# Routing and list matmuls in the routing's own PSUM bank, list steps on VectorE, weight preparation off GpSimd

## The chip, the cores and the metric

The kernel runs on one core of one Trainium2 chip. The metric is the device time of one execution in microseconds. PE is TensorE, DVE is VectorE, ACT is ScalarE, POOL is GpSimd, SP is SyncE (it issues most DMAs).

## The reference

Three parts follow one another. Attention over 4 batches and 8 heads gives x, 2304 tokens by 512. A gated hidden layer gives x2 = ((x·w1) * (x·w2))·w3·w_out, with 1024 hidden units. Then each token goes to one of 8 experts, at most 288 tokens each, in the order of all logits:

```python
logits = x @ w_gate
order = np.argsort(-logits.flatten())
for idx in order:
    tok, e = divmod(int(idx), E)
    if assigned[tok] >= 0 or counts[e] >= cap:
        continue
    assigned[tok] = e
    counts[e] += 1
for e in range(E):
    out[assigned == e] = np.maximum(x[assigned == e] @ w1[e], 0) @ w2[e]
```

The matrices are multiplied as two parts, a rounded high one and the rest (`xhi`, `xlo`, `wh`, `wl`), in three matmuls: high·high, low·high, high·low.

## The kernel before

Attention takes the first 511 us. From 512 to 775 us lies the hidden layer ("h"): for each of 8 slices of 128 hidden units, `weights` (line 1241) prepares w1 and w2, `split_x` (line 1255) splits x, and `hidden` (line 1289) forms a·b. A weight arrives as 64-bit words. `convert` rebuilds it in 128x512 pieces (`cv_raw`, `cv_v`): one DVE tensor_scalar, two DVE bit operations, one POOL multiply (a square, 40 of them in the program), and a DVE compare against `LEAST` squared that puts tiny values to zero. `split` then rounds the high part on ACT or DVE and subtracts the low part on DVE or POOL, whichever a planner finds free. Beside the h slices run the steps of `project` (`wo`, `og`), the product of the gate with the later weights, from which the logits come.

From 723 to 821 us PE forms W = w3·w_out (`pb<-wo,w`), and from 821 to 940 us x2 = h·W in 18 tiles of 128 tokens, each 24 matmuls of 512 columns. The last LATE = 3 tiles are made in two halves of 256 columns; the left halves first, so that expert 0's tokens can be gathered early. From 945 us the experts run: gather, first layer (e1), second layer (e2), scatter.

Between these matmuls run the routing and the lists. `routing` (line 872) has 8 phases. In each of the first 7 it looks for a threshold in 4 rounds; a round is a chain that alternates between DVE and PE: DVE makes `rt_mask`, PE counts (`rt_oh,rt_mask`, three matmuls), DVE makes `rt_cnt` and `rt_own`, PE adds over partitions (`rt_own,rc_ones`), DVE reduces. After the fourth round come `rt_rows` (PE: `rc_neg`, `rc_neg`, `rc_tri`), a scan, `rt_y`, and the choice of tokens that ends in the next `rt_oh`. `slot_lists` (line 1098) then makes one expert's list of tokens beside the next phase's first round: `sl_all`, `sl_rows`, a matmul with `rc_tris`, `sl_pre`, the slot of each token, `sl_oh` (one-hot rows, 3 DVE operations of 128x576), `sl_mv`, and 18 matmuls whose stationaries are 96 columns of `sl_oh`.

What sets the order: class `Sched` (line 163) plans all engines before the program is built, from modelled durations and priorities; each engine then runs its list in order. Small DVE temporaries of routing and lists lie in one PSUM bank (`in_bank`, line 853), named pt_68 in the order's rows. The results of routing and list matmuls go to one of three other PSUM tiles, pt_65 to pt_67 ("slots", through `Hold`), which the transposes of gathered tokens use as well. The trace writes all four as `pt`. Line 113 is the helper through which most instructions are recorded.

Of the kernel before, what the change touches and what calls it, by code (L numbers as in the profile page):

```python
# [775 lines left out]
def routing_consts(nc, pool, spare):  # L776
# [69 lines left out]
    c["g4"] = g4 = pool.tile([128, 4], F32, name="rc_first")  # L846
    nc.gpsimd.iota(g4, pattern=[[96, 4]], base=1, channel_multiplier=0, allow_small_or_imprecise_dtypes=True)
# [24 lines left out]
def routing(nc, sch, rp, slots, bank, c, L, keyL, A, rows_of, idx, prio, prio_l):  # L872
# [6 lines left out]
    def ring(name, n, shape, dt):  # L879
        return make_ring(sch, rp, "rt_" + name, n, shape, dt)  # L880
# [16 lines left out]
    r_al, r_acc, r_s = at("al", 1, [128, 8], F32), ring("acc", 1, [128, 8, NC], F32), at("s", 1, [128, NC], F32)  # L897
# [29 lines left out]
    for ph in range(8):  # L927
# [19 lines left out]
        if ph < 7:  # L947
# [4 lines left out]
            for rd, b in enumerate(BITS):  # L952
# [19 lines left out]
                ps = Hold(slots)  # L972

                def f(ps=ps, mask=mask, oh=oh):
# [17 lines left out]
                ps = Hold(slots)  # L992
                sch.op("PE", 110, lambda ps=ps: nc.tensor.matmul(
                    ps.tile[:, 0:NTHR * 8], c["ones16"], own8.rearrange("p t e -> p (t e)"), start=True, stop=True), r=["own8", "own8r"],
                    takes=ps, prio=prio, slack=RT_SLACK)
                dve(NTHR * 8, lambda ps=ps, any_=any_: nc.vector.tensor_reduce(
                    any_, ps.tile[:, 0:NTHR * 8].rearrange("p (t e) -> p t e", e=8), axis=AX.X, op=OP.max), [], [kany], uses=[ps])
# [32 lines left out]
            ps = Hold(slots)  # L1030

            def f(ps=ps, rows=rows):
                nc.tensor.matmul(ps.tile[:, 0:8], c["neg"], rows[:, 0:8], start=True, stop=True)
                nc.tensor.matmul(ps.tile[:, 8:16], c["neg"], rows[:, 0:8], start=True, stop=False)
                nc.tensor.matmul(ps.tile[:, 8:16], c["tri"], rows[:, 8:16], start=False, stop=True)
            sch.op("PE", 40, f, r=[kro], takes=ps, prio=prio)
# [9 lines left out]
            sch.op("DVE", c_dve(8), lambda ps=ps, r2=r2: nc.vector.tensor_tensor(r2, ps.tile[:, 0:8], rem, op=OP.add),  # L1046
                   r=[keyR], uses=[ps], w=[kr2], prio=prio)
# [4 lines left out]
            sch.op("DVE", c_dve(8), lambda ps=ps, al=al: nc.vector.scalar_tensor_tensor(  # L1052
                al, ps.tile[:, 8:16], 1e6, rem, op0=OP.add, op1=OP.add), r=[keyR], uses=[ps], w=[kal], prio=prio)
# [8 lines left out]
            ac2, kac2 = r_acc()  # L1062
# [6 lines left out]
            dve(144, lambda ac2=ac2: nc.gpsimd.tensor_tensor(A, A, ac2, op=OP.add), ["A", kac2], ["A"], "POOL")  # L1069
# [28 lines left out]
def slot_lists(nc, sch, rp, slots, bank, c, A, idx, prio, prio_l):  # L1098
# [8 lines left out]
    r_inc, r_pre, r_slot = ring("inc", 2, [128, NC], F32), ring("pre", 2, [128, 1], F32), at("slot", 2, [128, NC], F32)  # L1107
    r_ge, r_g, r_r = ring("ge", 2, [128, NC, 4], F32), ring("g", 2, [128, NC], F32), at("r", 1, [128, NC], F32)
    r_oh, r_og = ring("oh", 1, [128, NC, 96], BF16), ring("og", 1, [128, NC, 3], F32)
    r_mv, r_fl = ring("mv", 2, [128, 2, 3, NC], BF16), ring("fl", 2, [96, 2, 3], F32)  # L1110

    def lists(n, own):
# [15 lines left out]
        ps = Hold(slots)  # L1128
        sch.op("PE", 60, lambda: nc.tensor.matmul(ps.tile[:, 0:1], c["tris"], rows, start=True, stop=True),
               r=[kr], takes=ps, prio=prio_l)  # L1130
        dve(36, lambda: nc.vector.tensor_tensor_scan(inc, c["rst"][:, 0, :], s, 0.0, op0=OP.mult, op1=OP.add), [ks], [ki])
        dve(1, lambda: nc.vector.tensor_copy(pre, ps.tile[:, 0:1]), [], [kp], uses=[ps])
        dve(18, lambda: nc.vector.scalar_tensor_tensor(slot, inc, pre, s, op0=OP.add, op1=OP.mult), [ki, kp, ks], [ksl])
        dve(72, lambda: nc.vector.tensor_tensor(
            ge, slot[:, :, None].to_broadcast([128, NC, 4]), c["g4"][:, None, :].to_broadcast([128, NC, 4]), op=OP.is_ge),
            [ksl], [kg])
        dve(54, lambda: nc.vector.tensor_reduce(g, ge[:, :, 0:3], axis=AX.X, op=OP.add), [kg], [kc])
        dve(18, lambda: nc.vector.scalar_tensor_tensor(r, g, -96.0, slot, op0=OP.mult, op1=OP.add), [kc, ksl], [krr])
        for x in range(3):
# [13 lines left out]
        sch.op("PE", 18 * 60, f2, r=[(ko, x) for x in range(3)] + [(km, x) for x in range(2)], takes=ps2, prio=prio_l, slack=LIST_SLACK)  # L1153
        dve(6, lambda: nc.vector.tensor_copy(fl.rearrange("p x g -> p (x g)"), ps2.tile[:96, 0:6]), [], [kf], uses=[ps2])
# [14 lines left out]
def moe_and_experts(tc, sch, env, w1, w2, w3, w_out, w_gate, e1, e2, out):  # L1169
# [44 lines left out]
    def convert(w, row, col, blocks, width, pr):  # L1214
# [3 lines left out]
        if w.dtype != mybir.dt.int64:  # L1218
# [95 lines left out]
    def logits(f, c, pr):  # L1314
# [4 lines left out]
        split(lambda: hh[:, :], lambda: hl[:, :], lambda: hraw[:, f, cs], LC, pr, h_keys(f, c * LC, LC), khh, khl)  # L1319
# [20 lines left out]
    def project(nm, weight, copy, rows_n, cols, stat, stat_key, put_hi, put_lo, dst_key, step):  # L1340
# [4 lines left out]
        for t in range(n):  # L1345
            ac = slice(128, 256)
            for h in range(cols // DM):
                pr = P_WG + WG_STEP * (step + t * (cols // DM) + h)
                v, kv = convert(weight, t * 128, h * DM, 1, DM, pr)
                if nm == "og":  # L1350
# [3 lines left out]
                                   key, (key, 1), free=free))  # L1354
# [148 lines left out]
    r_xo = ring(xr, "x2o", 3, [128, DM], F32)  # L1503
# [268 lines left out]
LATE = 3  # L1772
# [57 lines left out]
```

## Time and profile before

| | |
|---|---|
| time, median of 3 runs | 1218.14 us (1217.03 to 1221.08) |
| profiled execution | 1218.05 us, its span 1216.1 us |
| mean granted clock of PE | 0.986 of full speed |
| busy: PE, DVE, ACT, POOL | 95%, 80%, 54%, 50% of the span |
| chain that ended last | PE 77%, DVE 15%, DMA 3%, issue 2% |

PE is busy for 1159.5 us of the span and idle for 56.6 us. A row of the timeline gives start, duration, engine, line, the operation and, in brackets, how long the engine was idle just before and what ended that. Matmuls overlap, so the distance of two starts says more than a duration.

### The profile page before, as it was taken

How to read it: one execution, taken by the hardware profiler on the slowest of the kernel's cores; microseconds unless marked ns; L12 is line 12 of the kernel's file. 1: busy time of each engine (PE TensorE's matmuls, PEld its weight loads, DVE VectorE, ACT ScalarE, POOL GpSimd, SP SyncE). 2: the span in 40 equal slices, each digit the busy share in tenths (PEclk: the TensorE clock that was granted, in tenths of full speed). 3: DMA queues.
4: the chain of work that ended last, by engine and by line, in shares of the span. 5: the costliest groups of instructions: out<-in, count | busy, mean ns of one | idle time of the engine just before them, and what ended most of it. 6: DMA issues, size and time to landing. Idle time of an engine off the chain costs nothing.

```text
span 1216.1 us, 24258 instructions
## 1 busy us (share of the span) xinstructions
PE 1159.5 (95%) x8377; PEld 1093.1 (90%) x8377; DVE 976.6 (80%) x2930; ACT 655.7 (54%) x1365; POOL 613.9 (50%) x645
## 2 busy tenths in 40 slices
PE   7999999999999999889999999999999799899996
PEld 6899999999999999879999999877768799899996
DVE  8899999999999999998777777677777877867541
ACT  6788888888888888642222220214222454444520
POOL 4566666666666665644423334323443368766110
PEclk9999999999999999999999999999999799999998
DMA  8576666666666653125455542544112564445520
GB/s 210 141 175 156 155 158 143 154 158 145 154 143 154 159 115 87 39 87 183 174 180 176 175 146 70 158 159 137 37 44 50 168 213 160 164 145 168 190 71 20
DMA packets 114217, 167.91 MB, mean 138 GB/s; under 512 B 47479, under 2 KB 77310, under 8 KB 114094
## 3 DMA queue, kind: packets, MB, share of 16 engines
q1 hardware_dynamic: 110926, 156.92, 47.5%
q0 software_dynamic: 3168, 9.44, 2.5%
q8 instruction: 66, 1.08, 0.4%
q14 instruction: 57, 0.47, 0.1%
HBM read 104.87 MB, written 22.48 MB: 105 GB/s over the span
## 4 chain that ended last, share of the span: by engine, by line
PE 77%; DVE 15%; DMA 3%; issue 2%; SPq 1%; POOL 1%; ACT 1%; DVEq 0%; POOLq 0%; ACTq 0%
PE pb L113 37%; PE s L590 12%; PE pt L614 7%; PE pt L664 6%; PE pt L113 6%; PE s L664 5%; DVE pt L113 3%; PE s L614 3%; DVE cv_v L113 2%; DMA u<-in_moe_w_dram 1%; DVE p L600 1%; DVE p_lo L648 1%; PE pt L543 1%; DVE sl_oh L113 1%; DMA cv_raw<-in_moe_w_dram 1%
## 5 line engine op out<-in xcount | busy, mean ns | idle before, releaser
L600 DVE TENSOR_SCALAR_CACHE_REDUCE p<-s 128x384 f32<-128x384 f32 x432 | 229.8, 550 | 35.9 <-PE s L590 12.3
L590 PE MATMUL s<-kst,qst 128*128 128x384 f32 x768 | 200.8, 361 | 5.5 <-DVE p L600 3.1
L605 ACT ACTIVATE p<-p,mn 128x1152 f32<-128x1152 f32 x144 | 181.1, 1258 | 26.1 <-DVE mn L603 23.9
L113 PE MATMUL pb<-xhi,wh 128*128 128x288 f32 x512 | 155.4, 304 | 1.7 <-ACT wh L113 1.7
L113 PE MATMUL pb<-xlo,wh 128*128 128x288 f32 x512 | 151.3, 296 | 4.0 <-DVE xlo L113 3.8
L113 PE MATMUL pb<-xhi,wl 128*128 128x288 f32 x512 | 150.9, 295 | 1.4 <-DVE wl L113 1.4
L590 PEld LDWEIGHTS s<-kst,qst 128*128 128x128 f32 x768 | 124.3, 192 | 11.4 <-DVE p L600 7.6
L614 PE MATMUL pt<-ident,p 128*128 128x128 f32 x879 | 132.1, 272 | 0.3 <-ACT p L605 0.3
L648 DVE TENSOR_TENSOR p_lo<-pt,p_hi 128x384 fp32r<-128x384 f32 x230 | 124.5, 551 | 0.8 <-ACT p_hi L331 0.7
L331 ACT ACTIVATE p_hi<-pt 128x384 fp32r<-128x384 f32 x230 | 106.6, 493 | 11.9 <-PE pt L614 10.2
L614 PEld LDWEIGHTS pt<-ident,p 128*128 128x128 f32 x879 | 106.8, 140 | 4.4 <-ACT p L605 0.5
L113 DVE SCALAR_TENSOR_TENSOR cv_v<-cv_raw,cv_v 128x512 int32<-128x512 int32 (+1 forms) x120 | 102.1, 856 | 7.1 <-POOL cv_raw L113 4.9
L113 PEld LDWEIGHTS pb<-xlo,wh 128*128 128x128 f32 x512 | 96.2, 188 | 5.0 <-DVE xlo L113 4.9
L113 PEld LDWEIGHTS pb<-xhi,wh 128*128 128x128 f32 x512 | 96.1, 188 | 2.5 <-ACT wh L113 1.9
L113 PEld LDWEIGHTS pb<-xhi,wl 128*128 128x128 f32 x512 | 96.1, 188 | 1.8 <-DVE wl L113 1.8
L341 POOL TENSOR_TENSOR p_lo<-praw,p_hi 128x384 fp32r<-128x384 f32 x96 | 96.8, 1016 | 0.4
L113 ACT ACTIVATE a<-pb 128x288 f32<-128x288 f32 x64 | 26.3, 410 | 131.3 <-PE pb L113 125.1
L335 POOL CAST p_hi<-praw 128x384 fp32r<-128x384 f32 x96 | 47.5, 505 | 84.8 <-ACT praw L331 84.8
L113 POOL TENSOR_TENSOR ul<-u,uh 128x1024 fp32r<-128x1024 f32 (+1 forms) x41 | 77.1, 1904 | 21.8 <-ACT uh L113 21.8
L113 POOL TENSOR_TENSOR cv_raw<-cv_raw 128x512 f32<-128x512 f32 x40 | 43.2, 1079 | 87.0 <-DVE cv_v L113 67.8
L113 PE MATMUL pb<-exh,uh 128*128 128x288 f32 x248 | 79.9, 322 | 0.0
L113 PE MATMUL pb<-ehh,uh 128*128 128x288 f32 x256 | 79.4, 310 | 0.0
(316 smaller groups left out, 3293.7 us busy)
## 6 DMA issues: line engine op xcount, KB each, us to landing
u<-in_moe_w_dram SPq DMA_DIRECT2D x64, 512.0 KB, 3.7
cv_raw<-in_moe_w_dram SPq DMA_DIRECT2D x32, 512.0 KB, 4.1
vr<-in_v_dram SPq DMA_DIRECT2D x32, 288.0 KB, 5.5
kr<-in_k_dram SPq DMA_DIRECT2D x32, 288.0 KB, 5.7
kst<-kH SPq DMA_DIRECT2D x31, 288.0 KB, 3.9
kst<-kL SPq DMA_DIRECT2D x31, 288.0 KB, 5.4
qr<-in_q_dram SPq DMA_DIRECT2D x15, 576.0 KB, 5.3
w3t<-wg SPq DMA_DIRECT2D x16, 512.0 KB, 3.5
```

The source lines that it names most:

```text
L113: return f(*[x.get() if isinstance(x, Lazy) else x for x in a], **{n: x.get() if isinstance(x, Lazy) else x for n, x in k.items()})
L331: nc.scalar.activation(out, in_, AF.Copy)
L335: nc.gpsimd.tensor_copy(out, in_)
L341: (nc.vector if eng == "DVE" else nc.gpsimd).tensor_tensor(out, a, b, op=OP.subtract)
L543: nc.tensor.transpose(ps.tile[:, a * 128:(a + 1) * 128], r[:, 3 * c + a, :, :].rearrange("p h d -> p (h d)"), ident)
L590: nc.tensor.matmul(ps.tile[:, :384], a[:, :], b[:, cs], start=(n == 0), stop=(n == len(passes) - 1))
L600: sch.op("DVE", c_dve(384), lambda ps=ps, c=c, cs=cs: nc.vector.tensor_scalar(t[:, cs], ps.tile[:, :384], 1.0, BIG, op0=OP.mult, op1=OP.mi ...
L605: sch.op("ACT", c_act(S, psum=False, acc=True), lambda: nc.scalar.activation(t, t, AF.Exp, bias=mn[:, 3:4], scale=-1.0, accum_out=sm[0][:, ...
L614: nc.tensor.transpose(ps.tile[:, a * 128:(a + 1) * 128], t[:, b * 128:(b + 1) * 128], ident)
L648: sch.op("DVE", c_dve(384), lambda view=view, src=src: nc.vector.tensor_tensor(view(lo), src(), view(hi).bitcast(F32), op=OP.subtract), us ...
L664: nc.tensor.matmul(ps.tile[:, :n], vt[:, t, :, :], src[half][:, t, off:off + n], start=(half == 0 and t == 0), stop=(half == 1 and t == NT ...
```

## The change

- `convert`: the POOL square becomes an absolute value on ACT; the compare is against `LEAST`.
- Splits of the hidden layer, of `wo` and of h: high parts on ACT only, low parts on DVE only (the first slice's `wl` and the first batch's `xlo` may still go to POOL, the first batch's `xhi` to DVE). `project` starts with the second slice, at a rate of 0.6 steps per chunk rather than 0.5.
- LATE is 4 rather than 3.
- List steps: the addition to `A`, `og` and the two `sl_mv` go from POOL to DVE; `sl_ge` has 54 elements rather than 72 and reads two SBUF tiles; `sl_oh` gets 32 zero columns, and each of the 18 list matmuls reads 128 columns.
- All routing and list matmuls write into the routing's bank rather than into a slot.

```diff
 # routing
-                ps = Hold(slots)
-                        nc.tensor.matmul(ps.tile[0:NCG * NTHR, 0:NCG * 8], mask[:, gs, :].rearrange("p a t -> p (a t)"),
+                pc, kpc = r_pcnt()
+                        nc.tensor.matmul(pc, mask[:, gs, :].rearrange("p a t -> p (a t)"),
...
+            pr_, kpr = r_prows()
+                nc.tensor.matmul(pr_[:, 0:8], c["neg"], rows[:, 0:8], start=True, stop=True)
...
-            dve(144, lambda ac2=ac2: nc.gpsimd.tensor_tensor(A, A, ac2, op=OP.add), ["A", kac2], ["A"], "POOL")
+            dve(144, lambda ac2=ac2: nc.vector.tensor_tensor(A, A, ac2, op=OP.add), ["A", kac2], ["A"])
 # slot_lists
+        pb, kpb = r_before()
+        sch.op("PE", 60, lambda: nc.tensor.matmul(pb, c["tris"], rows, start=True, stop=True),
...
-        dve(54, lambda: nc.gpsimd.tensor_tensor(og, ge[:, :, 0:3], ge[:, :, 1:4], op=OP.subtract), [kg], [kog], engine="POOL")
+        dve(54, lambda: nc.vector.tensor_tensor(
+            og, g[:, :, None].to_broadcast([128, NC, 3]), c["g4"][:, None, 3:6].to_broadcast([128, NC, 3]), op=OP.is_equal), [kc], [kog])
...
-                nc.tensor.matmul(ps2.tile[:96, 0:6], oh[:, k, :], mv[:, :, :, k], start=(k == 0), stop=(k == NC - 1))
+                nc.tensor.matmul(pl[:, :], oh[:, k * 96:k * 96 + 128], mv[:, :, :, k], start=(k == 0), stop=(k == NC - 1))
 # convert, split, project
-        sch.op("POOL", c_pool(n), lambda: nc.gpsimd.tensor_tensor(
-            raw[:, :, 0].bitcast(F32), raw[:, :, 1].bitcast(F32), raw[:, :, 1].bitcast(F32), op=OP.mult), r=[kv], w=[kr], prio=pr)
+        sch.op("ACT", c_act(n, False), lambda: nc.scalar.activation(raw[:, :, 0].bitcast(F32), raw[:, :, 1].bitcast(F32), AF.Abs),
...
-        split(..., khh, khl)
+        split(..., khh, khl, hi_e=("ACT",), lo_e=("DVE",))
...
-            if int((f * NCH + c + 1) * WG_RATE) > int((f * NCH + c) * WG_RATE):
+            if f and int((f * NCH + c + 1) * WG_RATE) > int((f * NCH + c) * WG_RATE):
...
-PRE_UNITS, MAIN_UNITS, LG_LAG, WG_RATE = 4, 9, 6, 0.5
+PRE_UNITS, MAIN_UNITS, LG_LAG, WG_RATE = 4, 9, 6, 0.6
-LATE = 3
+LATE = 4
```

The order on the engines changes with it, from the hidden layer on; attention's stays, but for its last operations. First the second list on DVE, at the first round's count; what an instruction waits for stands in brackets, pt_65 to pt_67 are the slots and pt_68 is the routing's bank. Before:

```order
L113 SCALAR_TENSOR_TENSOR rows_10030<-pt_68,rc_row 128x4 [waits DVE_49]
L113 TENSOR_TENSOR rt_pend_9186<-rt_pend_9186,pt_68 128x8
L113 TENSOR_TENSOR sl_all_9586<-A,pt_68 128x144 [waits Pool_49]
L113 TENSOR_TENSOR rt_cnt_9245<-pt_67,rc_diag 90x48 [waits PE_49]
L113 TENSOR_REDUCE pt_68<-sl_all_9586 128x18 [waits DVE_49]
L113 TENSOR_REDUCE pt_68<-rt_cnt_9245 90x8 [waits DVE_49]
L113 TENSOR_REDUCE sl_rows_10046<-pt_68 128x1 [waits DVE_49]
L113 SCALAR_TENSOR_TENSOR sl_inc_10048<-rc_rst,pt_68 128x18
L113 TENSOR_TENSOR rt_own_9188<-pt_68,rc_thr 90x120
L113 COPY sl_pre_10055<-pt_66 128x1 [waits PE_49]
L113 SCALAR_TENSOR_TENSOR pt_68<-sl_inc_10048,sl_pre_10055,pt_68 128x18 [waits DVE_49]
L113 TENSOR_TENSOR sl_ge_10062<-pt_68,rc_first 128x72 [waits DVE_49]
```

and in the changed kernel:

```order
L113 SCALAR_TENSOR_TENSOR rows_10033<-pt_68,rc_row 128x4 [waits DVE_49]
L113 TENSOR_TENSOR rt_pend_9188<-rt_pend_9188,pt_68 128x8 [waits PE_49]
L113 TENSOR_TENSOR sl_all_9591<-A,pt_68 128x144
L113 TENSOR_TENSOR rt_cnt_9249<-pt_68,rc_diag 90x48
L113 TENSOR_REDUCE pt_68<-sl_all_9591 128x18 [waits DVE_49]
L113 TENSOR_REDUCE pt_68<-rt_cnt_9249 90x8 [waits DVE_49]
L113 TENSOR_REDUCE sl_rows_10051<-pt_68 128x1 [waits DVE_49]
L113 SCALAR_TENSOR_TENSOR sl_inc_10054<-rc_rst,pt_68 128x18
L113 TENSOR_TENSOR rt_own_9190<-pt_68,rc_thr 90x120
L113 COPY sl_pre_10060<-pt_68 128x1 [waits PE_49]
L113 SCALAR_TENSOR_TENSOR sl_slot_10064<-sl_inc_10054,sl_pre_10060,pt_68 128x18 [waits PE_49]
L113 TENSOR_REDUCE pt_68<-pt_68 128x15 [waits DVE_49]
```

The order is the same, but `rt_pend` and the slot's operation, which touch the bank and use no result of PE, now wait for PE as well: the first for the count, the second for the sum of `rt_own`.

Next PE at the change from x2 to expert 0, the fourth list. Before:

```order
L113 LDWEIGHTS rt_mask_9215
L113 MATMUL pt_65<-rt_oh_9232,rt_mask_9215 90x48
L113 LDWEIGHTS rc_ones_145
L113 MATMUL pt_67<-rt_own_9188,rc_ones_145 128x120 [waits DVE_49]
L113 LDWEIGHTS rc_tris
L113 MATMUL pt_66<-sl_rows_10046,rc_tris 128x1 [waits DVE_49]
L113 MATMUL pt_65<-ident,early 128x96 [waits DMASW0_49]
L113 MATMUL pt_65<-ident,early 128x96 [waits DMASW1_49]
```

and in the changed kernel:

```order
L113 LDWEIGHTS rt_mask_9221
L113 MATMUL pt_68<-rt_oh_9236,rt_mask_9221 90x48
L113 LDWEIGHTS rc_tris
L113 MATMUL pt_68<-sl_rows_10051,rc_tris 128x1 [waits DVE_49]
L113 LDWEIGHTS rc_ones_145
L113 MATMUL pt_68<-rt_own_9190,rc_ones_145 128x120 [waits DVE_49]
L113 MATMUL pt_65<-ident,early 128x96 [waits DMASW0_49]
L113 MATMUL pt_65<-ident,early 128x96 [waits DMASW1_49]
```

The matmuls on `sl_rows` and `rt_own` have changed places and now write to pt_68; the transposes of `early` follow as before.

Last POOL from the end of attention into the hidden layer. Before:

```order
L113 TENSOR_TENSOR cv_raw_6159<-cv_raw_6159 128x512
L113 TENSOR_TENSOR cv_raw_6191<-cv_raw_6191 128x512
L738 TENSOR_TENSOR x_101<-x_101,rs_207 128x576
L113 MEMSET wg_hl 128x1408
L113 TENSOR_TENSOR xlo_6573<-x_94,xhi_6564 128x576
L113 TENSOR_TENSOR cv_raw_6159<-cv_raw_6159 128x512
L113 TENSOR_TENSOR cv_raw_6191<-cv_raw_6191 128x512
L113 TENSOR_TENSOR hl_6625<-hraw,hh_6601 128x384
L113 TENSOR_TENSOR wl_6639<-cv_v_6300,wh_6628 128x512
L113 TENSOR_TENSOR hl_6660<-hraw,hh_6633 128x384
```

and in the changed kernel:

```order
L113 TENSOR_TENSOR wl_6457<-cv_v_6301,wh_6450 128x512
L738 TENSOR_TENSOR x_101<-x_101,rs_208 128x576
L113 MEMSET wg_hl 128x1408
L113 TENSOR_TENSOR x2l_9186<-hraw,x2h_9172 128x512 x2
L113 TENSOR_TENSOR x2l_9233<-hraw,x2h_9195 128x512
L113 TENSOR_TENSOR Wl<-wt_9215,Wh 128x512
```

The squares (`cv_raw`) and the `hl`, `xlo` and `wl` of this stretch are gone from POOL, but for one `wl`; its next work after `wg_hl` is that of x2 and W.

## Rows read from the trace of the kernel before

**Rows 1.** Windows: busy of PE, PEld, DVE, ACT, POOL; clock; DMA share; GB/s.

```profile
512.00:548.00 36.00, 29.27 (x209) 27.35 (x210) 34.84 (x48) 14.01 (x27) 19.38 (x14) 1.00 0.27 90
775.00:821.00 46.00, 43.75 (x215) 32.84 (x215) 33.38 (x139) 9.65 (x16) 15.00 (x15) 1.00 0.53 170
821.00:906.00 85.00, 79.29 (x416) 59.80 (x416) 63.95 (x251) 27.12 (x47) 35.21 (x34) 1.00 0.28 75
906.00:975.00 69.00, 59.04 (x422) 53.09 (x421) 53.54 (x180) 25.21 (x45) 25.63 (x25) 0.90 0.37 108
```

**Rows 2.** Waits of PE, 511 to 548 us: total us, times, longest us.

```profile
PE pb L113 <- DVE xlo L113: 3.8, 3, 1.7
PE pb L113 <- ACT wh L113: 1.7, 1, 1.7
PE pb L113 <- DVE wl L113: 1.4, 2, 1.1
```

**Rows 3.** Waits of PE, 775 to 1216 us, the same columns.

```profile
PE pt L113 <- DVE rt_oh L113: 6.8, 6, 2.0
PE pt L113 <- DVE rt_mask L113: 6.0, 6, 3.3
PE pt L113 <- DVE exl L113: 5.0, 3, 2.6
PE pt L113 <- DVE sl_rows L113: 3.5, 4, 1.7
PE pt L113 <- DVE rt_own L113: 2.8, 3, 2.0
```

**Rows 4.** Groups of DVE, 505 to 546 us: busy, mean ns, idle before.

```profile
L113 DVE SCALAR_TENSOR_TENSOR cv_v<-cv_raw,cv_v 128x512 int32<-128x512 int32 x12 | 13.1, 1100 | 0.1
L113 DVE CAST xhi<-x 128x576 fp32r<-128x576 f32 x3 | 3.8, 1267 | 0.0
```

**Rows 5.** Timeline of DVE, one instruction of that stretch: start us, us, instruction.

```profile
508.34 0.69 DVE L113 SCALAR_TENSOR_TENSOR cv_v<-cv_raw,cv_v 128x512 int32<-128x512 int32 x1
```

**Rows 6.** Timeline of DVE around the second list: start us, us, instruction, [idle before <-releaser].

```profile
851.62 0.20 DVE L113 TENSOR_TENSOR rt_cnt<-pt,rc_diag 90x48 f16<-90x48 f32 x1 [0.63 <-PE pt L113]
...
855.79 0.30 DVE L113 SCALAR_TENSOR_TENSOR rt_y<-rt_ge,pt 128x144 f32<-128x144 f32 x1
...
856.01 0.16 DVE L113 TENSOR_TENSOR rt_r<-pt,rt_rem 128x8 f32<-128x8 f32 x1
...
860.51 0.29 DVE L113 TENSOR_TENSOR rt_oh<-rt_t,pt 128x144 bf16<-128x144 f32 x1
...
861.52 0.16 DVE L113 SCALAR_TENSOR_TENSOR rows<-pt,rc_row 128x4 int32<-128x4 f32 x1
...
862.92 0.25 DVE L113 TENSOR_TENSOR rt_own<-pt,rc_thr 90x120 f16<-90x120 f32 x1
...
868.07 0.44 DVE L113 TENSOR_TENSOR rt_mask<-pt,rt_thr 128x270 bf16<-128x270 f32 x1
```

**Rows 7.** Timeline of PE in the same stretch.

```profile
855.52 0.20 PE L113 MATMUL pt<-rt_rows,rc_neg 128*128 128x8 bf16 x2
...
860.85 0.27 PE L113 MATMUL pt<-rt_oh,rt_mask 128*90 128x48 bf16 x3 [0.85 <-DVE rt_oh L113]
...
862.96 0.16 PE L113 MATMUL pt<-sl_rows,rc_tris 128*128 128x1 bf16 x1 [0.61 <-DVE sl_rows L113]
...
867.11 0.95 PE L113 MATMUL pt<-sl_mv,sl_oh 128*96 128x6 bf16 x18
...
868.56 0.31 PE L113 MATMUL pt<-rt_oh,rt_mask 128*90 128x48 bf16 x3 [0.50 <-DVE rt_mask L113]
```

**Rows 8.** Weight loads of two tiles: ns min/median/max, starts, forms.

```profile
L113 PEld LDWEIGHTS <-sl_oh x144: 121/126/197, 822.5 to 1114.0; 128*96 128x96 bf16 x144
L113 PEld LDWEIGHTS <-rc_neg x14: 95/98/101, 811.1 to 1092.7; 128*128 128x128 bf16 x14
```

**Rows 9.** Timeline of DVE, one instruction of the fifth list.

```profile
1060.20 3.75 DVE L113 SCALAR_TENSOR_TENSOR idx<-sl_fl 96x3 int32<-96x3 f32 x1
```

More of the change, by code (lines that the diff above doesn't have):

```diff
@@ L991, in routing @@
                     c["thr"][:, :, None].to_broadcast([NCG * NTHR, NTHR, 8]), op=OP.mult), [ksm], ["own8"])
[L992 to L997, printed above, removed]
+                pa, kpa = r_pany()
+                sch.op("PE", 110, lambda pa=pa: nc.tensor.matmul(
+                    pa, c["ones16"], own8.rearrange("p t e -> p (t e)"), start=True, stop=True), r=["own8", "own8r"],
+                    w=[kpa], prio=prio, slack=RT_SLACK)
+                dve(NTHR * 8, lambda pa=pa, any_=any_: nc.vector.tensor_reduce(
+                    any_, pa.rearrange("p (t e) -> p t e", e=8), axis=AX.X, op=OP.max), [kpa], [kany])
                 dve(NTHR, lambda any_=any_, flag=flag: nc.vector.tensor_scalar(flag, any_, 0.0, None, op0=OP.is_ge), [kany], [kf])
@@ L1029, in routing, with f @@
             dve(288, f, [(kge, 0), (kge, 1)], [kro])
[L1030 to L1036, printed above, removed]
+            pr_, kpr = r_prows()
+            def f(pr_=pr_, rows=rows):
+                nc.tensor.matmul(pr_[:, 0:8], c["neg"], rows[:, 0:8], start=True, stop=True)
+                nc.tensor.matmul(pr_[:, 8:16], c["neg"], rows[:, 0:8], start=True, stop=False)
+                nc.tensor.matmul(pr_[:, 8:16], c["tri"], rows[:, 8:16], start=False, stop=True)
+            sch.op("PE", 40, f, r=[kro], w=[kpr], prio=prio, slack=RT_SLACK)
             inc, kin = r_incp()
@@ L1127, in lists @@
         dve(18, f, [ks], [kr])
-        ps = Hold(slots)
-        sch.op("PE", 60, lambda: nc.tensor.matmul(ps.tile[:, 0:1], c["tris"], rows, start=True, stop=True),
-               r=[kr], takes=ps, prio=prio_l)
+        pb, kpb = r_before()
+        sch.op("PE", 60, lambda: nc.tensor.matmul(pb, c["tris"], rows, start=True, stop=True),
+               r=[kr], w=[kpb], prio=prio_l, slack=LIST_FIRST)
         dve(36, lambda: nc.vector.tensor_tensor_scan(inc, c["rst"][:, 0, :], s, 0.0, op0=OP.mult, op1=OP.add), [ks], [ki])
-        dve(1, lambda: nc.vector.tensor_copy(pre, ps.tile[:, 0:1]), [], [kp], uses=[ps])
+        dve(1, lambda: nc.vector.tensor_copy(pre, pb), [kpb], [kp])
         dve(18, lambda: nc.vector.scalar_tensor_tensor(slot, inc, pre, s, op0=OP.add, op1=OP.mult), [ki, kp, ks], [ksl])
-        dve(72, lambda: nc.vector.tensor_tensor(
-            ge, slot[:, :, None].to_broadcast([128, NC, 4]), c["g4"][:, None, :].to_broadcast([128, NC, 4]), op=OP.is_ge),
+        dve(54, lambda: nc.vector.tensor_tensor(
+            ge, slot[:, :, None].to_broadcast([128, NC, 3]), c["g4"][:, None, 0:3].to_broadcast([128, NC, 3]), op=OP.is_ge),
             [ksl], [kg])
-        dve(54, lambda: nc.vector.tensor_reduce(g, ge[:, :, 0:3], axis=AX.X, op=OP.add), [kg], [kc])
+        dve(54, lambda: nc.vector.tensor_reduce(g, ge, axis=AX.X, op=OP.add), [kg], [kc])
         dve(18, lambda: nc.vector.scalar_tensor_tensor(r, g, -96.0, slot, op0=OP.mult, op1=OP.add), [kc, ksl], [krr])
@@ L1246, in weights @@
             split(lambda wh=wh, x=x: wh[:, x].rearrange("p k c -> p (k c)"), lambda wl=wl, x=x: wl[:, x].rearrange("p k c -> p (k c)"),
-                  lambda v=v: v.bitcast(F32), 512, pr, [kv], (kwh, x), (kwl, x))
+                  lambda v=v: v.bitcast(F32), 512, pr, [kv], (kwh, x), (kwl, x), hi_e=("ACT",), lo_e=("DVE", "POOL") if sch.label == "cv" else ("DVE",))
         return (wh, kwh), (wl, kwl)
@@ L1259, in split_x @@
             hi, free = xhi[i]
-            pages.first(sch.op(None, {"ACT": c_act(SP, False), "DVE": c_dve(SP, fast=True)},
+            pages.first(sch.op(None, {"ACT": c_act(SP, False)} | ({"DVE": c_dve(SP, fast=True)} if b == 0 else {}),
                                lambda eng, i=i, hi=hi: evac(eng, hi[:, :], xT[i][:, :]), r=[("x", b, k)], w=[("xhi", b, k)] + free,
                                prio=pr))
-            sch.op(None, {"DVE": c_dve(SP), "POOL": c_pool(SP)}, lambda eng, i=i, k=k, lo=lo, hi=hi: sub(
+            sch.op(None, {"DVE": c_dve(SP)} | ({"POOL": c_pool(SP)} if b == 0 else {}), lambda eng, i=i, k=k, lo=lo, hi=hi: sub(
                 eng, lo[:, k, :], xT[i][:, :], hi[:, :].bitcast(F32)), r=[("x", b, k), ("xhi", b, k)], w=[("xlo", b, k)], prio=pr)
@@ L1318, in logits @@
         hl, khl = r_hl()
-        split(lambda: hh[:, :], lambda: hl[:, :], lambda: hraw[:, f, cs], LC, pr, h_keys(f, c * LC, LC), khh, khl)
+        split(lambda: hh[:, :], lambda: hl[:, :], lambda: hraw[:, f, cs], LC, pr, h_keys(f, c * LC, LC), khh, khl, hi_e=("ACT",), lo_e=("DVE",))
         o0 = LW - 16 - 16 * c
@@ L1353, in project @@
                     tt.first(split(lambda hl=hl: hl[:, 0, :], lambda hl=hl: hl[:, 1, :], lambda v=v: v.bitcast(F32), DM, pr, [kv],
-                                   key, (key, 1), free=free))
+                                   key, (key, 1), hi_e=("ACT",), lo_e=("DVE",), free=free))
                     store(copy[t], hl, [key, (key, 1)], [(nm, "f", t)], pr)
```

64 lines of the change are left out of this document (36 added, 28 removed).

## The prediction

> **What bounds the kernel now.** I read the stages first, by windows, then what PE waited for, then the timeline of one list. PE is busy nearly everywhere, so what counts is where it is not. In 512 to 548 us, the start of the hidden layer, PE works 29.3 of 36 us while DVE works 34.8 of them [rows 1]: DVE bounds that stretch. PE waits there 3.8 us for `xlo`, 1.7 for `wh`, 1.4 for `wl`, together 6.9 [rows 2]. From 775 us on the routing's chain shows: PE is idle for 2.3, 5.7 and 10.0 us in the three next windows, and in the last of these its granted clock is 0.90 [rows 1]. The waits for `rt_oh`, `rt_mask`, `sl_rows` and `rt_own` make 6.8 + 6.0 + 3.5 + 2.8 = 19.1 us; expert 0's tokens (`exl`) make 5.0 [rows 3]. Those 19.1 us lie almost all beside lists: a plain round is covered by the matmuls placed around it.
>
> **The change, part by part.**
>
> *Start of the hidden layer.* Twelve DVE bit operations took 1.10 us on average there, three casts of `xhi` 1.27 us each [rows 4], while the same bit operation with POOL idle took 0.69 us [rows 5]. POOL's squares and low parts leave the stretch, so 12 x 0.41 = 4.9 us come off DVE, and the casts, 3.8 us, go to ACT. Against that DVE gets POOL's few low parts, each about the size of one bit operation: five of them are 3.5 us. DVE comes out some 5 us ahead in a stretch where PE waited 6.9 us for it. The later start of `project` takes DVE work out as well, which I count against the weight chain that no longer overlaps. I take -5.5 us; the ends are 0 (the chain to the first `wh` is one of latency) and -6.9 (all waits gone). Later in this layer DVE has room, and what moves to it and to ACT costs nothing; if that cover were gone it would show as waits for `hl` or `wl`.
>
> *List matmuls of 128 columns.* A list's 18 matmuls take 0.95 us [rows 7], and their weight loads of 96 columns 126 ns each, where a load of 128 columns takes 98 ns [rows 8]. By that ratio a list takes 0.74 us: 8 x 0.21 = 1.7 us saved. The ends are 0 and half of the 0.95, 3.8 us in all. I take -1.7, the row's own ratio. The Trainium skill, "TensorE: Matmul & The Clock Gate", section "Weight-path perf modes — Fast Weight Load (FWL) and DoubleRow", says that loads become about twice as fast where there are 128 weight columns and the type is not fp32. The trace agrees in sign (98 ns against 126 ns); by the factor of two the term would be -3.8 us, and the sum 1225.
>
> *One bank.* In the changed order a PE matmul that writes to the routing's bank waits for the last DVE instruction before it that touches this bank, and the next DVE instruction that touches it waits for the matmul, whether or not the data are related. In a plain round the chain alternates anyway and nothing is added. Beside a list two chains share the bank. I work the second list through:
> - The matmuls on `rt_rows` started at 855.52 us and their reader `rt_r` at 856.01, hidden by the scan before `rt_y` [rows 6, 7]. Now they wait for the scan's end (about 855.76) and `rt_y` waits for them: PE stalls 0.3 us, and `rt_y` starts at 856.3 rather than 855.79, 0.5 later.
> - The addition to `A` on DVE: 0.3 us, as `rt_y`, which has the same size [rows 6].
> - The count behind `rt_oh` waits for `rows`, which ends at 861.68 rather than 860.80 [rows 6]: 0.9 later. So the count moves from 860.85 to 862.55. PE has one x2 matmul more before it (18 took 4.4 us between 855.6 and 860.0, 0.24 each [rows 7]). Its wait grows from 0.85 to 2.0 us.
> - Then `rt_pend` waits for the count, 0.63 us as `rt_cnt` did [rows 6]; from the end of `rows` to that of `rt_own` it was 1.5 us, so `sl_rows` finds PE idle for 0.65 us, as before (0.61 [rows 7]).
> - `sl_pre` waits for that matmul, the matmul on `rt_own` waits for `sl_pre` (PE idle 0.45), and the slot waits for that one: two trips of 0.63 us that were hidden. From the end of `rt_own` to that of `rt_mask` it was 5.3 us [rows 6]; with 1.3 for the trips and 0.65 for `og` and two `sl_mv` (each like a small DVE row, 0.16 to 0.25) it is 7.25. PE has 20 matmuls, 4.7 us, instead of 15 and the list: it waits 1.65 rather than 0.50 us.
> - The next `rt_cnt` waits for the whole list, with three matmuls behind it on PE: about 0.5 us.
>
> Together 0.3 + 2.0 + 0.65 + 0.45 + 1.65 + 0.5 = 5.55 us of stalls instead of 1.96, so +3.5 a list. Three lists lie beside W and x2: +10.5. At the fourth, PE has 15 matmuls of 256 columns before the count instead of 23, and none between count, `sl_rows` and `rt_own`; some of the `exl` waits should go, as slots come free and the early gather has four tiles of right halves for cover instead of three. Net +2.5. At the fifth and sixth the matmuls of the experts are the cover; I take +2 each. The last two have no rounds beside them: 0. Sum +17; the ends are 0 and 7 x 3.5 = +24.5. DVE is the waiting engine each time; behind its waits stand the splits of x2 or of the experts, and PE waits for these no sooner than for the routing.
>
> The Trainium skill, "PSUM — Partial Sum Buffer", section "PSUM bank collisions raise a hardware error", says that the compiler's scheduler adds a dependency between any two instructions of different engines on the same bank and quadrant, reads and writes alike. The changed order agrees, as `sl_slot` waits for PE. Without that rule only `A`, `og` and `sl_mv` would be longer, about 7 x 1 us, and the sum would be 1218.
>
> *The rest.* LATE = 4 gives a few more matmuls of half width, too little to count, and a longer cover, -1 us. One DVE operation on 96x3 numbers took 3.75 us [rows 9] and made the longest `rt_mask` wait, 3.3 us [rows 3]; it and POOL's work beside it stay, so I count 0 for it, with 3.3 us to either side.
>
> Sum, from the profiled execution of 1218.05 us, practically the median of 1218.14: 1218.05 - 5.5 - 1.7 + 17 - 1 = 1226.9. I forecast **1227 us**.
>
> **Rivals.**
> - *The waits are mostly covered.* PE loses only half of the 17 us, as other work stands before the waiting matmuls, while all of the 6.9 us at the start, the 3.8 of the lists and the 5.0 of `exl` go: 1218.05 + 8.5 - 6.9 - 3.8 - 5.0 = 1211. For it: the waits before were all under 2 us but for two, and the order was planned anew. Against it: the plan left 5 matmuls between count and `sl_rows`, as before.
> - *It cancels.* The first three lists cost 2 us each and the others 1.2 in all, 7.2, as much as the first two parts bring: 1218.
> - *The clock falls too.* In 906 to 975 us there were 10 us of stalls, and the clock of 0.90 took 69 x 0.10 = 6.9 us more [rows 1]. If the 17 us of stalls are followed by the same share: 1227 + 11.7, about 1238. Against it: 821 to 906 has 5.7 us of stalls at full clock [rows 1].
> - *The start of the hidden layer brings nothing*, since ACT's chain replaces POOL's: 1232.
>
> **How the numbers follow.** Forecast 0.40, covered 0.25, cancels 0.13, clock 0.12, nothing at the start 0.10. Faster, same and slower, by 0.3% (3.7 us, about what a measurement here can tell from none): 0.25, 0.13, 0.62. The range goes from the covered case to the clock's, 1210 to 1238; the forecast's own range is 1221 to 1233.
>
> **What would show it.** After the change PE's waits at 512 to 548 us should be under 2 us and the bit operations near 0.7 us; a list's 18 matmuls 0.5 to 0.75 us; the second list's first count should follow a PE wait of about 2 us, ended by `rows`, its second one of 1.6, ended by `sl_mv`; a PE wait should stand before the matmul on `rt_own`. PE's waits after 775 us should sum to some 40 us rather than 26. If these waits are below 1 us in the x2 window, the forecast is wrong.

## The result, and the profile after

The changed kernel takes 1225.46 us (median of 6 runs, 1223.24 to 1227.23) where the kernel before took 1219.28 us beside it (6 runs, 1214.96 to 1221.08). The ratio is 1.0057, with a 95% interval of 1.0034 to 1.0081; runs beside the experiments gave 1.0073 (1.0060 to 1.0087). It is slower, by 6 to 9 us; the forecast was 1227 us, 9 us slower.

The profiled execution took 1227.12 us, its span 1225.3. Where its time stands against the kernel before is best read from the starts of a few PE instructions in the two timelines; a stretch runs from one such start to the next. (The hidden layer began at 512.8 us before and at 510.9 after, though attention is the same; other profiles of unchanged attention had 508.9 to 514.5, so stretches are compared, not times from the span's start. W, the product with `wo`, starts at 770.7 us in the kernel before, not at 723.)

| stretch, from its first PE instruction | us before | us after | PE idle before | after |
|---|---|---|---|---|
| hidden layer | 257.96 | 252.07 | 6.65 | 2.31 |
| W to the first `rt_rows` | 40.33 | 40.97 | 0.76 | 0.94 |
| list 1 (to the next `rt_rows`) | 44.45 | 46.66 | 3.07 | 3.77 |
| list 2 | 40.09 | 42.90 | 1.96 | 2.82 |
| list 3, with the late tiles | 41.67 | 45.33 | 2.66 | 3.21 |
| list 4, to expert 0 | 61.01 | 65.15 | 9.48 | 14.66 |
| list 5 | 47.44 | 47.70 | 1.55 | 4.50 |
| list 6 | 46.91 | 48.23 | 5.02 | 4.79 |
| the rest | 114.43 | 116.37 | 2.29 | 4.95 |

The hidden layer is 5.9 us shorter. All that follows is 17.0 us longer, although each list's matmuls are shorter. The changed order moves some matmuls across the marks: after the change list 2 has two more of 512 columns (some 0.5 us), list 5 has 12 fewer of 288 columns and list 6 has 12 more (some 1.4 us), so lists 5 and 6 are best read together.

The start of the hidden layer, by windows (the columns of [rows 1]; the first window begins 1 us earlier than in [rows 1]):

```profile
511.00:548.00 37.00, 34.69 (x255) 33.76 (x256) 33.69 (x58) 20.25 (x39) 4.16 (x3) 1.00 0.30 95
821.00:906.00 85.00, 79.21 (x386) 59.03 (x385) 61.65 (x246) 22.30 (x39) 32.21 (x25) 0.96 0.24 63
```

PE waits there 2.6 us in all, where the waits of [rows 2] make 6.9, and none of it for `xlo`. POOL, the fifth figure, works 4 us instead of 19 [rows 1]. The bit operations that took 1100 ns [rows 4] have this row in the groups of DVE, 505 to 546 us:

```profile
L113 DVE SCALAR_TENSOR_TENSOR cv_v<-cv_raw,cv_v 128x512 int32<-128x512 int32 x15 | 11.5, 770 | 0.1
```

The second row of the windows is of x2: as many PE-busy us as in [rows 1], but 386 matmuls instead of 416, and a granted clock of 0.96 instead of 1.00. Of the 30 that are missing, 18 are those of list 1, which now lies ahead of 821 us, but 6 are x2's own. In this window PE is idle no longer than before (5.8 us), it is slower: at 0.96 it loses 3.4 us of 85. What PE waited for from 755 us on, against [rows 3]:

```profile
PE pt L113 <- DVE rows L113: 8.5, 5, 1.9
PE pt L113 <- DVE pt L113: 8.2, 5, 4.2
PE pt L113 <- DVE rt_own L113: 7.8, 9, 1.9
PE pt L113 <- DVE sl_inc L113: 2.7, 2, 2.3
PE pt L113 <- DVE sl_mv L113: 2.2, 3, 1.4
```

`rt_oh` no longer releases the first count: `rows`, three operations later, does. `pt` is an operation of DVE on the bank whose result the waiting matmul does not read. The second list on PE and on DVE, as timelines ([rows 7] and [rows 6] show the same before):

```profile
850.58 0.19 PE L113 MATMUL pt<-rt_rows,rc_neg 128*128 128x8 bf16 x2
...
857.11 0.27 PE L113 MATMUL pt<-rt_oh,rt_mask 128*90 128x48 bf16 x3 [1.90 <-DVE rows L113]
...
859.16 0.16 PE L113 MATMUL pt<-sl_rows,rc_tris 128*128 128x1 bf16 x1 [0.56 <-DVE rt_own L113]
...
859.73 0.32 PE L113 MATMUL pt<-rt_own,rc_ones 97*128 97x120 f16 x1
...
866.01 0.27 PE L113 MATMUL pt<-rt_oh,rt_mask 128*90 128x48 bf16 x3
866.12 0.63 PE L113 MATMUL pt<-sl_mv,sl_oh 128*128 128x6 bf16 x18
866.60 0.47 PE L113 MATMUL pb<-Wl,x2h 128*128 128x512 f32 x1
```

```profile
857.41 0.16 DVE L113 TENSOR_TENSOR rt_pend<-rt_pend,pt 128x8 f32<-128x8 f32 x1 [0.36 <-PE pt L113]
...
859.36 0.16 DVE L113 COPY sl_pre<-pt 128x1 f32<-128x1 f32 x1 [0.25 <-PE pt L113]
...
860.09 0.23 DVE L113 SCALAR_TENSOR_TENSOR sl_slot<-sl_inc,sl_pre,pt 128x18 f32<-128x18 f32 x1 [0.57 <-PE pt L113]
...
865.58 0.38 DVE L113 TENSOR_TENSOR sl_mv<-pt,rc_ids 128x54 bf16<-128x54 f32 x1
866.78 0.20 DVE L113 TENSOR_TENSOR rt_cnt<-pt,rc_diag 90x48 f16<-90x48 f32 x1 [0.83 <-PE pt L113]
```

The wait ahead of the first count is 1.90 us (forecast 2.0), and DVE now waits for PE at `rt_pend`, `sl_pre`, the slot and `rt_cnt`. Ahead of the second count there is no wait, where 1.65 us were forecast. The reason stands in a window of that moment:

```profile
859.50:862.50 3.00, 3.00 (x8) 2.22 (x8) 2.19 (x11) 0.63 (x1) 0.25 (x1) 0.50 0.11 24
```

After the wait of 1.90 us and the one of 0.56, PE's clock was granted at 0.50 (1.2 GHz) for 3.4 us, so that the same matmuls lasted until DVE was ready: 1.7 us were lost in busy time instead of in a wait. (In `after_again`, a second profile of the changed kernel, the wait ahead of this count is there, 1.30 us, and the low stretch follows it; the list then takes 43.98 us, 1.1 more.) Such stretches between 500 us and the kernel's last matmuls cost 17.1 us in the profile after and 11.9 before, by windows of half a microsecond. How the loss divides changes from profile to profile: `after_again` has 41.4 us of idle time from W on and 13.7 from low clock, this one 39.6 and 17.1. The row of the list has a duration of 0.63 us where it was 0.95 [rows 7]. Both include the end of the last matmul: from the first start of a list to the next instruction, where that follows at once, it is 0.48 us after (866.12 to 866.60 above) and 0.81 before:

```profile
1108.65 0.95 PE L113 MATMUL pt<-sl_mv,sl_oh 128*96 128x6 bf16 x18
1109.46 0.38 PE L113 MATMUL pb<-ehh,uh 128*128 128x288 f32 x1
```

So 0.33 us a list are saved, 2.6 us at eight. Their loads after the change:

```profile
L113 PEld LDWEIGHTS <-sl_oh x144: 95/96/112, 819.4 to 1124.0; 128*128 128x128 bf16 x144
```

### The profile page after: what moved, and what is told of

Its sections match the earlier page's. It is cut to its first block, busy times and chain, and to the rows that moved or that the text cites. A ratio compares the mean times of both kernels' runs of the same rounds, so it can differ in the third digit from the quotient of the medians.

```text
span 1225.3 us, 24269 instructions
## 1 busy us (share of the span) xinstructions
PE 1160.0 (95%) x8401; PEld 1094.3 (89%) x8401; DVE 960.6 (78%) x2961; ACT 702.6 (57%) x1456; POOL 501.9 (41%) x530
## 3 DMA queue, kind: packets, MB, share of 16 engines
q8 instruction: 66, 1.08, 0.4%
## 4 chain that ended last, share of the span: by engine, by line
PE 80%; DVE 13%; DMA 3%; issue 2%; SPq 1%; ACT 1%; POOL 0%; DVEq 0%; POOLq 0%; ACTq 0%
PE pb L113 37%; PE s L590 12%; PE pt L614 7%; PE pt L113 6%; PE pt L664 6%; PE s L664 5%; DVE pt L113 4%; PE s L614 3%; DMA u<-in_moe_w_dram 1%; DVE sl_oh L113 1%; DVE p L600 1%; PE pt L543 1%; DVE cv_v L113 1%; DMA vr<-in_v_dram 1%; DMA kr<-in_k_dram 0%
## 5 line engine op out<-in xcount | busy, mean ns | idle before, releaser
L113 POOL TENSOR_TENSOR x2l<-hraw,x2h 128x512 fp32r<-128x512 f32 x36 | 46.6, 1300 | 314.4 <-PE pt L113 255.2
L590 PEld LDWEIGHTS s<-kst,qst 128*128 128x128 f32 x768 | 123.3, 190 | 12.9 <-DVE p L600 10.6
L113 DVE SCALAR_TENSOR_TENSOR cv_v<-cv_raw,cv_v 128x512 int32<-128x512 int32 (+1 forms) x120 | 83.7, 705 | 5.7 <-ACT cv_raw L113 4.5
L113 ACT ACTIVATE uh<-u 128x1024 fp32r<-128x1024 f32 (+1 forms) x84 | 68.4, 851 | 17.6 <-DMA u<-in_moe_w_dram 11.8
```

Of the source, the lines that this page charges most:

```text
L113: return f(*[x.get() if isinstance(x, Lazy) else x for x in a], **{n: x.get() if isinstance(x, Lazy) else x for n, x in k.items()})
L590: nc.tensor.matmul(ps.tile[:, :384], a[:, :], b[:, cs], start=(n == 0), stop=(n == len(passes) - 1))
```

## The experiments

Times are compared with runs of the kernel before on the same chip, whose median was 1216.3 to 1216.9 us each time. A run's kernel is planned anew, so each edit carries the order that the planner makes for it.

**The bank.** `a_slots` is the changed kernel with the slots back:

```diff
-                pc, kpc = r_pcnt()
+                ps = Hold(slots)
-                sch.op("PE", 200, f, r=[kma, koh], w=[kpc], ...)
+                sch.op("PE", 200, f, r=[kma, koh], takes=ps, ...)
```

and so for the other four results. 

> The changed kernel, but with the routing and list matmuls back in the three slots; list steps on VectorE, 128 columns, LATE = 4 and the new hidden layer stay. Theory 1 (the shared bank is what costs): the waits for rows, pt, sl_inc and sl_mv go, PE's waits after 775 us fall from 39.6 to about 26 us, the clock's low stretches fall from 8 to about 5, and the time is 1210 to 1213 us. Rival (the list steps on VectorE and the fourth late tile cost it, the bank is free): 1222 us or more.

It took 1208.83 us, ratio 0.9939 (0.9919 to 0.9958), a little better than theory 1 said. The changed kernel itself was run again beside the next kernels. 

> The changed kernel itself again, beside the others of this call, so that they can be compared with it on the same chip. Ratio to the kernel before 1.003 to 1.008, as it was.

It gave 1224.98 us, 1.0073. So the bank alone, with its order, costs 1.0073 / 0.9939, 1.3%, some 16 us (by the first ratio, 1.0057, 14). In the two profiles W and what follows take 434.6 us in `a_slots` and 452.4 in `after_again`: PE is idle for 31.4 us (about 26 were expected) instead of 41.4, and the low clock costs 5.1 us instead of 13.7. The two make up the whole difference. PE's waits from 755 us on in `a_slots`:

```profile
PE pt L113 <- DVE rt_oh L113: 8.3, 6, 3.5
PE pt L113 <- DVE rt_mask L113: 6.2, 6, 1.4
PE pt L113 <- DVE sl_rows L113: 4.3, 5, 1.6
PE pt L113 <- DVE exl L113: 2.7, 3, 1.0
```

The first four groups are those of [rows 3] again; `rows` and `sl_inc` have gone, and `sl_mv` is down to 0.2 us.

`b_bank` makes the same edit on the kernel before, in the other direction. 

> The kernel before with the routing and list matmuls in the routing's bank alone; to make room the flag and the slot of a token lie in SBUF. Theory 1: the bank's waits and the clock behind them cost 12 to 17 us: 1231 to 1236 us. Rival (the waits are a matter of the steps on VectorE): 1222 us or less.

It took 1240.32 us, ratio 1.0189 (1.0167 to 1.0211): 23 us slower, beyond what was expected. The sign is clear. In its profile, from W on, PE is idle 17.3 us longer than in the kernel before and the low clock costs 10.2 us more; why its waits are longer than the changed kernel's was not followed up. The largest group of waits in it is of the expected kind:

```profile
PE pt L113 <- DVE pt L113: 16.3, 10, 2.7
```

`a_pebank5` gives PE's results a bank, but not that of DVE's temporaries:

```diff
-    s_pt = Slots(env["pts"][:3])
+    bank2 = [env["pts"][2], 0]
+    s_pt = Slots(env["pts"][:2])
-AHEAD = 6
+AHEAD = 5
```

(all results are placed in `bank2`.) 

> The changed kernel, but all routing and list matmuls write to a PSUM tile of their own (the third slot's), in which VectorE keeps nothing; two slots are left for the transposes, and expert 0 borrows one of them rather than two. Theory 1 (the cost comes from VectorE's temporaries and the results in one bank, which tie unrelated work together): the waits for rows, pt and sl_inc go, about 1210 to 1214 us where the changed kernel has 1224. Rival (it comes from having one fixed place for results rather than three free ones): 1220 us or more.

1213.27 us, ratio 0.9980 (0.9961 to 0.9999): 0.9%, 11 us better than the changed kernel, with one slot less than `a_slots`. Sharing the place of the results with DVE's temporaries is most of the cost, then. The 4 us between this kernel and `a_slots` can be the fixed place, the missing slot or `AHEAD`; the run does not tell them apart. Its second list on PE, where the count is released by `rt_oh` again and waits 1.08 us rather than 1.90:

```profile
852.11 0.27 PE L113 MATMUL pt<-rt_oh,rt_mask 128*90 128x48 bf16 x3 [1.08 <-DVE rt_oh L113]
```

**The clock.** `a_fill` puts work into the wait:

```diff
                 def f(pc=pc, mask=mask, oh=oh, psd=psd):
+                    for _ in range(20 if psd else 0):
+                        nc.tensor.matmul(psd.tile[:, 0:128], c["neg"], c["tri"], start=True, stop=True)
```

with `psd` a slot, at lists 1 to 3. 

> The changed kernel with 20 idle-time matmuls (128 columns, results not used) on TensorE ahead of the first count beside lists 1 to 3, where it waits 1.9 us. Theory (the clock's low stretches of 3.4 us are a consequence of these waits): the three stretches that follow them go and the time falls by 3 to 5 us against the changed kernel. Rival (the low stretches come whatever TensorE does in the wait): the same time or up to 3 us more.

1221.97 us, ratio 1.0049 (1.0032 to 1.0066), beside 1.0073 (1.0060 to 1.0087): 2.9 us less, though 60 matmuls were added; the two intervals overlap by a little. The trace shows more. The wait at list 1 in `a_fill`, and then a window behind it:

```profile
808.25 1.29 PE L113 MATMUL pt<-rc_tri,rc_neg 128*128 128x128 bf16 x20
810.26 0.27 PE L113 MATMUL pt<-rt_oh,rt_mask 128*90 128x48 bf16 x3 [0.72 <-DVE rows L113]
```

```profile
812.00:815.00 3.00, 2.69 (x13) 2.17 (x13) 2.20 (x13) 0.00 (x0) 0.00 (x0) 1.00 0.76 246
```

and in the changed kernel, run beside it, the same moment:

```profile
811.50:814.50 3.00, 3.00 (x9) 2.23 (x8) 2.34 (x11) 0.00 (x0) 0.00 (x0) 0.50 0.58 209
```

None of the three low stretches that the changed kernel has beside lists 1 to 3 in `after_again` (from 811.5, 866.1 and 900.3 us, each of 3.4 us and a cost of 1.7) is there in `a_fill`. Of their 5.1 us lists 1 to 3 of the table got 2.5 back (134.6 us together in `after_again`, 132.1 in `a_fill`): at full clock PE is early at the second count and waits 1.3 us at each of the three lists, where the forecast, made without the clock, had 1.65.

**The list matmuls.** `b_128` is the kernel before with the 128-column loads:

```diff
-                nc.tensor.matmul(ps2.tile[:96, 0:6], oh[:, k, :], ...)
+                nc.tensor.matmul(ps2.tile[:, 0:6], oh[:, k * 96:k * 96 + 128], ...)
-        sch.op("PE", 18 * 60, f2, ...)
+        sch.op("PE", 18 * 27 + 60, f2, ...)
```

> The kernel before with stationaries of 128 columns in the list matmuls alone. In the changed kernel a list's 18 matmuls took 0.48 us rather than 0.95. Theory 1: 8 x 0.47 = 3.8 us saved, 1215.5 us. Rival: in the kernel before the list stands ahead of a matmul that waits for rt_mask anyway, so at four of eight lists the saving turns into a longer wait: about 1217.5 us, or 1219 if at all of them.

1210.11 us, ratio 0.9955 (0.9941 to 0.9969), 5.5 us: more than the 2.6 us that the lists can save (the 0.47 in my expectation compares a duration with a distance of starts). The list in it takes 0.49 us from its first start to the next instruction. The planner had been told a shorter duration and made another order, so `b_128o` keeps the old duration. 

> The kernel before with 128-column stationaries, but with the planner's old duration for the list's matmuls, so that the order is that of before. If the loads alone make the 5 to 6 us of the version with the new duration: 1210 to 1212 us. Rival (part of it is the new order, since in the old one the list stands ahead of a matmul that waits for rt_mask, and the saving turns into a longer wait): 1213 to 1216 us.

1213.23 us, ratio 0.9974 (0.9963 to 0.9985), 3.2 us. With the old order the wait behind the list grows, as the rival says; the second list on PE, to be read against 0.50 in [rows 7]:

```profile
862.89 0.64 PE L113 MATMUL pt<-sl_mv,sl_oh 128*128 128x6 bf16 x18
...
864.34 0.31 PE L113 MATMUL pt<-rt_oh,rt_mask 128*90 128x48 bf16 x3 [0.81 <-DVE rt_mask L113]
```

Here all of the second list's saving, 0.3 us, went into that wait. So it is at four of the eight lists in this profile, which stand ahead of a waiting matmul as in the kernel before; in the profile of `b_128` none does. The new order then has a part in the 5.5 us, but the two intervals overlap a little, and how large it is stays open.

**The hidden layer.** `b_hstage` is the kernel before with all edits of `convert`, the splits and the projection. 

> The kernel before with the new hidden layer alone (absolute value on ScalarE, high parts on ScalarE, low parts on VectorE, later start and rate of the projection). Theory 1: the 7.8 us that W starts earlier in the changed kernel stay to the end: 1211 to 1213 us. Rival (they are given back, as the routing's chain sets the pace from W on): 1217 us or more.

1210.90 us, ratio 0.9960 (0.9943 to 0.9976), 5 us; the hidden layer's stretch is 252.03 us, as in the changed kernel. (Of the 7.8 us in my expectation, 1.9 were only the earlier start of that profile's hidden layer.) `b_abs` has one part of it:

```diff
-        sch.op("POOL", c_pool(n), lambda: nc.gpsimd.tensor_tensor(raw..., raw..., raw..., op=OP.mult), ...)
+        sch.op("ACT", c_act(n, False), lambda: nc.scalar.activation(raw..., raw..., AF.Abs), ...)
```

> The kernel before with the absolute value on ScalarE in place of the square on GpSimd, and no other change. If GpSimd's multiplications beside VectorE's bit operations are what fills VectorE at the start of the hidden layer, most of the 5.5 us of the whole hidden-layer edit are here: 1212 to 1213 us. Rival (the splits and the later start of the projection bring it): 1215 us or more.

1216.27 us, ratio 0.9996 (0.9982 to 1.0009): nothing. The rows of its windows and groups show why; the first row is the same window in the kernel before, the second that in `b_abs`:

```profile
508.00:548.00 40.00, 32.35 (x234) 30.23 (x233) 38.68 (x54) 14.82 (x29) 20.53 (x15) 1.00 0.24 81
508.00:548.00 40.00, 32.36 (x221) 29.97 (x220) 38.74 (x55) 17.00 (x32) 18.97 (x12) 0.96 0.31 112
```

```profile
L113 DVE SCALAR_TENSOR_TENSOR cv_v<-cv_raw,cv_v 128x512 int32<-128x512 int32 x14 | 16.7, 1197 | 0.2
```

POOL, free of the squares, was given low parts instead by the planner and worked nearly as long as before, 19.0 us instead of 20.5. `b_pool` has everything but the projection's start and rate (`WG_RATE` 0.5, `WG_FIRST` 0, from the first slice on). 

> The kernel before with the absolute value on ScalarE and the fixed engines of the splits, but with the projection's start and rate as before: GpSimd is emptied in the hidden layer, and VectorE has the projection's work at its start. The absolute value alone brought nothing (GpSimd was still busy for 19 of 40 us at the start, with low parts, and the bit operations took 1.2 us), all three edits 5.5 us. If GpSimd being idle beside VectorE is what counts: bit operations near 0.77 us, PE's waits at the start 3 to 4 us, 1211 to 1213 us. Rival (the projection's later start brings it): 1215 us or more.

1215.57 us, ratio 0.9991 (0.9974 to 1.0007): again nothing that can be told from none, against my expectation. Its rows of the same two views:

```profile
508.00:548.00 40.00, 35.33 (x248) 32.81 (x247) 37.25 (x66) 22.47 (x42) 4.60 (x4) 0.96 0.34 114
```

```profile
L113 DVE SCALAR_TENSOR_TENSOR cv_v<-cv_raw,cv_v 128x512 int32<-128x512 int32 x14 | 10.8, 775 | 0.1
```

POOL is empty and the bit operations are fast, but PE waits for `og` and `hraw` instead (2.1 us up to 560 us), and a low clock follows, which costs 1.7 us. The layer is 256.8 us long. The 5 us come only when the projection's work leaves the start as well; whether that would do alone was not run.

**The rest, and a better version.** `g_best` is `b_hstage` with the edit of `b_128`. 

> The kernel before with the new hidden layer and the 128-column stationaries, and nothing else of the change. If the two gains add: 1216.4 - 5.5 - 4 to 6 = 1205 to 1207 us, faster than both kernels and than the changed kernel with slots (1208.8). If the list saving turns into waits once the hidden layer is shorter: 1210 us or more.

1204.53 us, ratio 0.9904 (0.9888 to 0.9920): the gains add, and it beats both kernels, by 12 and by 20 us. `a_slots3` is `a_slots` with `LATE = 3`, so that against `g_best` only the list steps on VectorE differ, with the small temporaries that the change moved for them. 

> The changed kernel with the results back in the slots and LATE = 3; against the new hidden layer with 128 columns alone (1204.5 us beside 1216.3) only the list steps on VectorE are left. Theory 1: the 4.3 us by which the version with slots and LATE = 4 lags (1208.8) are the list steps, which lie on the routing's chain (addition to A 0.3, og and two mv 0.65 us at seven lists, 6.6 in all, partly covered): 1207 to 1210 us. Rival: they are the fourth late tile, and this one is at 1204 to 1206 us.

1206.32 us, ratio 0.9915 (0.9897 to 0.9933). It lies between the two expectations. The list steps and the fourth late tile together cost about 4 us (0.9939 against 0.9904); how much each of them costs lies within the intervals and stays open.

## Why the prediction was right, step by step

The forecast, 1227 us and slower, came true, with the shared bank as the reason, as `a_slots`, `b_bank` and `a_pebank5` show. Its terms fared differently, and that the sum lies so near is in part luck. By ratios the hidden layer and the 128 columns together bring 11.7 us (`g_best`, 0.9904), where the forecast had 5.5 + 1.7 = 7.2; the bank, the list steps and LATE cost 20.6 us (1.0073 against 0.9904), where it had 17 - 1 = 16. The two errors, 4.5 us each, cancel.

- *Start of the hidden layer, -5.5 us.* The stretch lost 5.9 us and the edit alone brings 5 us. The size was right, the reason only half: I counted DVE's time beside POOL and set the projection's later start against the weight chain. `b_abs` and `b_pool` show that freeing POOL brings nothing measurable while the projection is at the start.
- *List matmuls, -1.7 us.* Mis-sized. Not the ratio of the load's durations counts (96 to 126 ns) but the distance of the starts: 0.81 to 0.48 us a list, 2.6 us in all, a factor of 1.7 where the row's ratio was 1.3. The factor of two that the Trainium skill gives ("TensorE: Matmul & The Clock Gate", section "Weight-path perf modes — Fast Weight Load (FWL) and DoubleRow") is nearer to it. `b_128`, 5.5 us, points to a gain from the new order on top.
- *One bank, +17 us, with the list steps on VectorE in it.* By runs the bank is some 16 us, and list steps and LATE, for which I took -1 by itself, another 4. In the trace, W and what follows are 17.0 us longer with the lists' 2.6 us saved, so the rest makes 19.6: idle time 12.9 (26.8 to 39.6), the clock 5.1 (11.9 to 17.1), and 1.6 that I cannot assign. The form was partly wrong. At the second list DVE waited 0.36, 0.25 and 0.57 us for PE at `rt_pend`, `sl_pre` and the slot, rather than 0.63 each time; the stall at `rt_rows` was 0.1 us rather than 0.3; and the matmul on `rt_own` did not wait, as an x2 matmul stands before it. Lists 1 to 3 were 2.2 to 3.7 us longer, 2.9 on average, instead of 3.5. Of these 8.7 us, 2.1 are idle time and some 6.8 are the four low stretches there, which the term did not have; a falling clock I had as a rival at 0.12. List 4 was 4.1 us longer (forecast 2.5), though the waits of `pt` for `exl` fell from 5.0 us [rows 3] to 0.7, as forecast; lists 5 and 6 together 1.6 (forecast 4), the rest 2 (forecast 0).
- *Sum of PE's waits.* I said some 40 us after 775 instead of 26. From W on they are 39.6 and 26.8.
- *The long DVE operation, 0.* It belongs to the sixth list, not the fifth. In the changed kernel it took 2.62 us instead of 3.75 and the wait of 3.3 us for `rt_mask` is gone, but PE is idle in this list for 4.79 us instead of 5.02: the 0 held.
- *Signs that did not come.* PE's waits at the start are 2.6 us, not under 2; the second list's second count has no wait, and its matmul on `rt_own` none.
- *A slip.* The 1218 for a bank without the dependency leaves out the -1; with it the sum is 1217. It changes no chance.
- *Rivals.* "Mostly covered" fell, as did "it cancels" (2.9 us a list rather than 2) and "nothing at the start" (5.9 us). "The clock falls too" was partly right, and is part of the term rather than an addition to it: when the clock falls behind a first wait, the next wait can disappear, as at the second list.

## What to carry to other kernels

In this kernel a PSUM bank that holds both one engine's temporaries and another's results tied the two in program order, related or not, and cost some 16 us: read in the built order what each of the engines waits for before you save a tile in this way. When an engine is to be relieved of a neighbour, look at what fills the neighbour's place: a planner that is free to choose put other work there (`b_abs`). Then look at what else the engine holds up: with the neighbour empty the bit operations fell to 775 ns, and the time did not (`b_pool`). The gain of this matmul chain showed in the distance of its starts, not in a load's duration, and a new duration in a planner's table is an edit of its own.

## What the runs showed of the hardware that I had not expected

Beside lists 1 to 3 of the changed kernel PE waited 1.85 to 1.90 us for the first count, and in both profiles a stretch of 3.4 us at half clock (0.50, 1.2 GHz) followed at each: at list 3 within 0.4 us, at list 1 after 1.0 and 2.3 us, at list 2 after a further wait, of 0.56 us in one profile and 1.30 in the other. In one of them a fourth stretch followed a wait of 1.36 us at list 3. With 20 small matmuls in the first wait, so that 0.7 us of it remained, there was no such stretch, though the later waits, 0.56 and 1.3 us, were still there. Nor was there one beside these lists of the kernel before, where PE waits 1.57 us at most. And with 128 columns of bf16 the matmuls of a list start every 27 ns instead of every 45, while a load's own duration only falls from 126 to 96 ns.
